# The last pair of blocks as seven products, its last product leaving its bank in groups of 128 tokens, the rest stored by column halves

## The chip, the cores and the metric

The kernel runs on one core of one Trainium2 chip. The metric is the device time of one execution in microseconds (us). "Span" is the length of one profiled execution as the trace shows it; it is 1.7 us shorter than the device time of the same execution (380.3 for 382.04 us before the change). Engines: PE is TensorE, DVE is VectorE, ACT is ScalarE, SP issues most of the stores (49 of 51 before the change). In this kernel a matmul's result is put into a bank of PSUM (`ps` in the traces), ACT or DVE copies it from there into an output tile in SBUF (`osb`), and a store, which is a DMA, takes it to `out_dram`. Semaphores are the counters by which the built program makes an engine wait for another engine or for a DMA. A store has landed when the last count of its semaphore has come in.

## The reference, cut

A gated recurrence along time, then a two-armed layer: the larger of two projections, and a projection of that.

```python
# x, f_logit: (4, 6144, 256); lower_bound: (256,); w1, w2: (256, 1024); w_out: (1024, 256)
f = lower_bound + (1 - lower_bound) * sigmoid(f_logit)
for t in range(S):
    h = f[:, t] * h + (1 - f[:, t]) * x[:, t]
    y[:, t] = h
out = np.maximum(y @ w1, y @ w2) @ w_out        # float32, (24576, 256)
```

## The kernel before

The 24576 tokens are 48 blocks of 512. The maximum is written as `w1·y + relu((w2 - w1)·y)`, so that a block's output is a sum over ten slices of 128: four slices of relu and one of `y` for each half `k` of the features. Two blocks `ja`, `jb` make a pair. With the ten slices in two halves (5 and 5) and the 256 output columns in two halves (`lo`, `hi`), a pair's output is a 2x2 by 2x2 matrix product, and all middle pairs do it with seven products instead of eight (Strassen's way). Each product is 20 matmuls of 128 columns: 4 groups of 128 tokens times 5 slices. The sums on the left side (`sum1` to `sum4`) are made by DVE from the relu's results.

This is the order of the seven, cut. `bank` is a bank of PSUM of 128x512 floats, `X`, `B` and `E` are three of them. `then` gives what follows a product's last matmul: `seed` and `snapshot` are copies by ACT, `leave` is a copy by ACT or a sum by DVE into the output tile.

```python
def sevenths(p):
    ...
    def seed(b, src):                       # new bank b = copy of bank src
        open_bank(b); nc.scalar.copy(out=bank[b][:], in_=bank[src][:])
    def snapshot(b, name):                  # to SBUF
        t = snpool.tile(...); nc.scalar.copy(out=t[:], in_=bank[b][:]); snap[name] = t
    def leave(b, j, cols, name, last):
        dst = osbs[j][:, :, cols]
        if name is None: nc.scalar.copy(out=dst, in_=bank[b][:])
        else: nc.vector.tensor_tensor(out=dst, in0=bank[b][:], in1=snap[name][:], op=ALU.add)
        if last: store(j, osbs[j])          # 512 KB, 4 KB pieces
    ...
    product("X", part(0, 0), plain(0, lo), True)
    then(seed("B", "X"))
    product("E", sub(1), given(t1), True)
    then(snapshot("E", 5))
    product("X", sub(2), given(t2))
    then(snapshot("X", 2))
    product("B", part(0, 1), plain(1, lo))
    then(leave("B", ja, lo, None, False))
    product("X", sub(3), given(t3))
    then(leave("X", jb, hi, 5, False))
    product("E", sub(4), plain(1, hi))
    then(leave("E", ja, hi, 2, True))
    product("X", part(1, 1), given(t4))
    then(leave("X", jb, lo, None, True))
```

A pair's products run in the gaps of the first layer of the next pair. The last pair has no next one, so the kernel before does it by the plain second layer, ten matmuls of 256 columns for each group. For the last block each group has a bank of its own and leaves at once:

```python
def second_layer(j, slot):
    ...
        if s == 0 and (r == 0 or j == NBLK - 1):
            acc["ps"] = ps_o.tile([P, 2, D], FP32, name="ps")     # a new bank
    ...
        if j == NBLK - 1 and s == n - 1:
            (nc.vector.tensor_copy if r else nc.scalar.copy)(
                out=osb[:, i : i + 1, :], in_=ps[:, r : r + 1, :])
            store(j, osb, i, 1, nc.sync if r else nc.scalar)      # 128 KB
...
for step in queue:                       # what is left of the pair before
    step()
for j in (NBLK - 2, NBLK - 1):
    for slot in range(FC):
        second_layer(j, slot)
```

## Time and profile before

| | before |
|---|---|
| device time, median of 4 runs | 382.45 us (382.36 to 382.71) |
| span of the profiled run | 380.3 us |
| PE busy | 97% of the span |
| last 80 matmuls (256 columns) | 367.20 to 376.12 us |
| last copy ends | 376.56 us |
| from there to the end | 3.70 us |

The page of the profile, part 4 (the chain of work that ended last, shares of the span):

```profile
PE 91%; DVE 6%; DMA 1%; ACT 0%; issue 0%; SPq 0%
```

PE is the bound. The end of that chain, as the chain of waits in order of time has it (start us, length us, what):

```profile
365.97 1.40 PE ps L605 x25
367.37 8.75 PE ps L482 x80
376.11 0.02 issue
376.14 0.42 DVE osb L491
```

In each line a group of instructions has its start, its length, its engine, the tile that it writes, its line of the kernel and its count. L605 is the matmul of the seven products, L482 that of the plain second layer. For 8.75 us PE does the last pair and nothing else; the change is about these 80 matmuls. From the timeline, the matmuls that give the rates (start us, length us, engine, line, operation, tiles, shapes, count):

```profile
366.09 1.28 PE L605 MATMUL ps<-t,r 128*128 128x128 f16 x20
367.20 0.38 PE L482 MATMUL ps<-w,r 128*128 128x256 f16 x2
...
376.14 0.42 DVE L491 COPY osb<-ps 128x256 f32<-128x256 f32 x1 [1.76 <-PE ps L482]
```

Twenty matmuls of 128 columns start within 1.11 us (366.09 to 367.20), 55.6 ns each. The costs of what stands around the products, from the page's groups (after the bar: busy us, mean ns of one):

```profile
L506 DVE TENSOR_TENSOR S<-r,S 128x2560 f16<-128x2560 f16 x42 | 62.0, 1477 | 0.0
L562 DVE TENSOR_TENSOR osb<-ps,sn 128x512 f32<-128x512 f32 x42 | 28.7, 684 | 6.5 <-ACT osb L560 5.3
L550 ACT COPY sn<-ps 128x512 f32<-128x512 f32 x42 | 24.6, 586 | 1.1 <-PE ps L605 1.1
```

So a late sum is 1.48 us, a sum out of a bank 0.68, a copy of a whole bank 0.59.

### The profile page before, as it was taken

To read this page: it belongs to the slowest core of one execution; us is meant where nothing else is said; L and a number is where in the kernel's file an instruction comes from. 1 tells how busy PE (TensorE), PEld (TensorE's weight loads), DVE (VectorE), ACT (ScalarE), POOL (GpSimd) and SP (SyncE) were. 2 spreads that over 40 slices of the span, in tenths; PEclk is the share of its full clock that TensorE was granted. 3 is DMA by queue.
4 is the path that set the end of the run, shared out by engine and by line. 5 is a ranking of instruction groups with operands and counts; after the bars stand their busy time and mean duration, and the time that the engine had idled before them with its cause. 6 is when DMAs were issued, how large, how long until landed. Compare 5 with 4: busy or idle time off the path is not lost.

```text
span 380.3 us, 9454 instructions
## 1 busy us (share of the span) xinstructions
PE 369.3 (97%) x4076; PEld 280.0 (74%) x4076; DVE 332.9 (88%) x402; ACT 300.4 (79%) x406; POOL 39.4 (10%) x79
## 2 busy tenths in 40 slices
PE   5999998999999999999999999999999999999995
PEld 4677766777777777777777777777777777777784
DVE  5685789999999999999999999999999999999721
ACT  5856797798798888888887887988888888888740
POOL 1500101110210110101201100202201101000000
PEclk9999999999999999999999999999999999999999
DMA  7995989999989999999999989999899999950223
GB/s 253 245 229 124 309 138 215 262 192 172 296 160 198 307 197 158 267 163 225 224 181 262 267 149 221 237 161 283 156 214 259 171 222 274 174 214 4 110 113 113
DMA packets 103389, 77.17 MB, mean 203 GB/s; under 512 B 93554, under 2 KB 94066, under 8 KB 102642
## 3 DMA queue, kind: packets, MB, share of 16 engines
q1 hardware_dynamic: 100514, 51.13, 60.0%
q0 software_dynamic: 2544, 25.17, 34.0%
q8 instruction: 32, 0.52, 0.6%
q10 hardware_dynamic: 288, 0.26, 0.2%
q14 instruction: 11, 0.09, 0.1%
HBM read 53.48 MB, written 48.23 MB: 267 GB/s over the span
## 4 chain that ended last, share of the span: by engine, by line
PE 91%; DVE 6%; DMA 1%; ACT 0%; issue 0%; SPq 0%
PE ps L605 42%; PE dT L436 41%; PE ps L482 6%; DVE r L230 1%; DVE S L506 1%; DMA osb<-in_f_logit_dram 1%; DVE wd L360 1%; PE ps L180 1%; DVE v L223 1%; DVE r L264 1%; DVE ff L213 0%; DVE t L415 0%; PE ps L392 0%; DVE osb L496 0%; ACT r L444 0%
## 5 line engine op out<-in xcount | busy, mean ns | idle before, releaser
L444 ACT ACTIVATE r<-dT 128x1024 f16<-128x1024 f32 x192 | 195.8, 1022 | 54.4 <-PE dT L436 54.3
L436 PE MATMUL dT<-r,wd 128*128 128x512 f16 x768 | 225.5, 379 | 1.1 <-ACT r L444 0.5
L605 PEld LDWEIGHTS <-S 128*128 128x128 f16 x1680 | 110.9, 101 | 38.6 <-DVE S L506 1.2
L605 PEld LDWEIGHTS <-r 128*128 128x128 f16 x1260 | 87.3, 101 | 36.6
L230 DVE TENSOR_TENSOR_SCAN r<-ff,r,v 128x512 f16<-128x512 f16 x88 | 108.2, 1271 | 0.8
L605 PE MATMUL ps<-t,S 128*128 128x128 f16 x1260 | 97.8, 219 | 1.0 <-DVE S L506 1.0
L436 PEld LDWEIGHTS <-wd 128*128 128x128 f16 x768 | 67.6, 113 | 6.5 <-issue 1.2
L506 DVE TENSOR_TENSOR S<-r 128x2560 f16<-128x2560 f16 x42 | 62.4, 1487 | 10.3 <-ACT r L444 10.3
L605 PE MATMUL ps<-wob,r 128*128 128x128 f16 x672 | 67.4, 219 | 0.0
L506 DVE TENSOR_TENSOR S<-r,S 128x2560 f16<-128x2560 f16 x42 | 62.0, 1477 | 0.0
L285 ACT ACTIVATE u<-fT 128x512 f16<-128x512 f16 x88 | 56.0, 637 | 0.6 <-DMA fT<-scr 0.6
L348 POOL CAST waited<-fT 128x1 f32<-128x1 f16 x21 | 13.6, 649 | 279.7 <-DMA fT<-scr 279.7
L213 DVE TENSOR_SCALAR ff<-u,nom 128x512 f16<-128x512 f16 (+1 forms) x98 | 31.4, 346 | 10.6 <-ACT u L207 6.7
L605 PE MATMUL ps<-w,r 128*128 128x128 f16 x168 | 36.8, 219 | 0.0
L562 DVE TENSOR_TENSOR osb<-ps,sn 128x512 f32<-128x512 f32 x42 | 28.7, 684 | 6.5 <-ACT osb L560 5.3
L605 PE MATMUL ps<-t,r 128*128 128x128 f16 x420 | 33.4, 219 | 0.0
L605 PE MATMUL ps<-wob,S 128*128 128x128 f16 x336 | 31.4, 219 | 0.0
L223 DVE TENSOR_TENSOR v<-u,xT 128x1024 f16<-128x1024 f16 x44 | 30.2, 686 | 0.0
L482 PEld LDWEIGHTS <-r 128*128 128x128 f16 x240 | 23.9, 101 | 6.9
L482 PE MATMUL ps<-wob,r 128*128 128x256 f16 x192 | 26.8, 273 | 0.0
L550 ACT COPY sn<-ps 128x512 f32<-128x512 f32 x42 | 24.6, 586 | 1.1 <-PE ps L605 1.1
L560 ACT COPY osb<-ps 128x512 f32<-128x512 f32 x42 | 24.4, 581 | 0.5 <-PE ps L605 0.5
(56 smaller groups left out, 134.3 us busy)
## 6 DMA issues: line engine op xcount, KB each, us to landing
out_dram<-osb SPq DMA_DIRECT2D x47, 512.0 KB, 3.8
scr<-in_f_logit_dram POOLq DMA_DIRECT2D x22, 512.0 KB, 7.8
scr<-in_x_dram POOLq DMA_DIRECT2D x22, 512.0 KB, 10.6
r<-in_moe_w_dram SPq DMA_DIRECT2D x4, 512.0 KB, 6.8
fT<-in_f_logit_dram POOLq DMA_DIRECT2D x3, 256.0 KB, 8.2
xT<-in_x_dram POOLq DMA_DIRECT2D x3, 256.0 KB, 9.7
osb<-in_f_logit_dram SPq DMA_DIRECT2D x2, 256.0 KB, 3.6
osb<-in_x_dram SPq DMA_DIRECT2D x2, 256.0 KB, 3.6
```

What stands on the lines that cost most here:

```text
L213: nc.vector.tensor_scalar(out=ff[:, h, cols], in0=u[:, h, cols], scalar1=nom[:, h : h + 1], scalar2=1.0, op0=ALU.mult, op1=ALU.add,)
L223: nc.vector.tensor_tensor(out=like(v[:, :, cols], xT), in0=like(u[:, :, cols], xT), in1=xT, op=ALU.mult,)
L230: nc.vector.tensor_tensor_scan(out=y_of(j, h), data0=ff[:, h, o : o + TB], data1=v[:, h, o : o + TB], initial=0.0 if t0 == 0 else y_of(j - ...
L285: nc.scalar.activation(out=mids[p + NBLK, "u"][:, h, cols], in_=held[c, 0][:, h, cols], func=AF.Sigmoid, scale=-1.0,)
L436: nc.tensor.matmul(dT[:, fc % 2, :], lhsT=wd[:, kc, unit_cols(fc)], rhs=y_of(j, kc), start=(kc == 0), stop=(kc == KC - 1),)
L444: nc.scalar.activation(out=rts[j, k][:, g - 1 : g + 1, :].rearrange("p q (i m) -> p q i m", m=P), in_=dT[:].rearrange("p q (m i) -> p q i ...
L482: nc.tensor.matmul(ps[:, r, :], lhsT=left, rhs=right, start=(s == 0 and (r == 0 or j == NBLK - 1)), stop=(s == n - 1 and (r == 1 or j == N ...
L506: nc.vector.tensor_tensor(out=t[:], in0=a, in1=b, op=op)
L550: nc.scalar.copy(out=t[:], in_=bank[b][:])
L560: nc.scalar.copy(out=dst, in_=bank[b][:])
L562: nc.vector.tensor_tensor(out=dst, in0=bank[b][:], in1=snap[name][:], op=ALU.add)
L605: nc.tensor.matmul(bank[b][:, i, :], lhsT=a[:, k, cols], rhs=w, start=fresh, stop=after is not None, skip_group_check=True,)
```

## The change

The intent: 140 matmuls of 128 columns in place of 80 of 256 (the work of seven eighths), with the end trimmed. Product B is moved forward, where it can run while DVE makes the sums; the last product leaves in four groups so that the last copy and store are small; the outputs of a half of the columns are stored as soon as they are there. Cut to its core:

```diff
     def sevenths(p):
+        end = p == NPAIR - 1
@@ leave
-                if last:
+                if end:
+                    store(j, osbs[j], cols=cols)          # 256 KB, 512 B pieces
+                elif last:
                     store(j, osbs[j])
+        def leave_group(b, j, cols, i):
+            def go():
+                copy, queue = (
+                    (nc.vector.tensor_copy, nc.sync),
+                    (nc.scalar.copy, nc.scalar),
+                )[i % 2]
+                copy(out=osbs[j][:, i, cols], in_=bank[b][:, i, :])
+                store(j, osbs[j], slice(i, i + 1), cols, queue)   # 64 KB
+            return go
@@ the seven
+        def first_out():
+            product("B", part(0, 1), plain(1, lo))
+            then(leave("B", ja, lo, None, False))
         product("X", part(0, 0), plain(0, lo), True)
         then(seed("B", "X"))
+        if end:
+            first_out()
         product("E", sub(1), given(t1), True)
         then(snapshot("E", 5))
         product("X", sub(2), given(t2))
         then(snapshot("X", 2))
-        product("B", part(0, 1), plain(1, lo))
-        then(leave("B", ja, lo, None, False))
+        if not end:
+            first_out()
         ...
         product("X", part(1, 1), given(t4))
-        then(leave("X", jb, lo, None, True))
+        if end:
+            for i in range(TB // P):                       # the last matmul of each group
+                steps[(i - TB // P + 1) * (KH + 1) - 1][-1] = leave_group("X", jb, lo, i)
+        else:
+            then(leave("X", jb, lo, None, True))
@@ sum3 of the last pair is made in the loop too; the tail of the kernel
-        for j in (NBLK - 2, NBLK - 1):
-            for slot in range(FC):
-                second_layer(j, slot)
+        steps = sevenths(p)
+        for step in steps[:20]:
+            step()
+        sum1(p); sum2(p); sum4(p)
+        for step in steps[20:]:
+            step()
```

The special cases for the last block in `second_layer`, its banks and its copies, go.

More of the change, by code (lines that the diff above doesn't have):

```diff
@@ L450, in first_layer, with store @@
             )
-    def store(j, osb, first=0, n=TB // P, queue=None):
+    def store(j, osb, groups=slice(0, TB // P), cols=slice(0, D), queue=None):
         b, t0, nb, c, o = blocks[j]
@@ L456, in store @@
             out=out[r0 : r0 + nb, :].rearrange("(p n) d -> p n d", p=P)[
-                :, first : first + n, :
+                :, groups, cols
             ],
-            in_=osb[:, first : first + n, :],
+            in_=osb[:, groups, cols],
         )
@@ L470, in second_layer @@
             g, r = divmod(i, 2)
-            if s == 0 and (r == 0 or j == NBLK - 1):
+            if s == 0 and r == 0:
                 acc["ps"] = ps_o.tile([P, 2, D], FP32, name="ps")
@@ L485, in second_layer @@
                 rhs=right,
-                start=(s == 0 and (r == 0 or j == NBLK - 1)),
-                stop=(s == n - 1 and (r == 1 or j == NBLK - 1)),
+                start=(s == 0 and r == 0),
+                stop=(s == n - 1 and r == 1),
                 skip_group_check=True,
             )
-            if j == NBLK - 1 and s == n - 1:
-                (nc.vector.tensor_copy if r else nc.scalar.copy)(
-                    out=osb[:, i : i + 1, :], in_=ps[:, r : r + 1, :]
-                )
-                store(j, osb, i, 1, nc.sync if r else nc.scalar)
-            elif r == 1 and s == n - 1:
+            if r == 1 and s == n - 1:
                 (nc.scalar.copy if j == 0 else nc.vector.tensor_copy)(
@@ L713 @@
             more = p + 1 < NPAIR
-            seq = [(27, scans[p]["scan10"]), (36, scans[p]["scan11"])]
+            seq = [
+                (27, scans[p]["scan10"]),
+                (36, scans[p]["scan11"]),
+                (112, lambda: sum3(p)),
+            ]
             if more:
@@ L721 @@
                     (84, scans[p + 1]["scan01"]),
-                    (112, lambda: sum3(p)),
                     (131, scans[p + 1]["decay1"]),
@@ L753 @@
             step()
-        for j in (NBLK - 2, NBLK - 1):
-            for slot in range(FC):
-                second_layer(j, slot)
+        p = NPAIR - 1
+        steps = sevenths(p)
+        for step in steps[:20]:
+            step()
+        sum1(p)
+        sum2(p)
+        sum4(p)
+        for step in steps[20:]:
+            step()
 _INS = ['x', 'f_logit', 'lower_bound', 'moe_w1', 'moe_w2', 'moe_w_out']
```

## The prediction

> **What bounds the kernel now.** TensorE: the chain of waits puts 91% of the 380.3 us span on PE. The tail is the last pair of blocks. In the timeline the seven-product work of the pair before ends with 20 matmuls of 128 columns from 366.09 us. Then 80 matmuls of 256 columns (the plain second layer) run from 367.20 to 376.12, 109 ns apart. The last copy (128x256, DVE, 0.42) ends at 376.56, the span 3.74 us later, with the last store. In the window 367 to 376 DVE is busy for 1.8 us, ACT for 1.3.
>
> **Removed and added on PE.** 80 x 109 ns = 8.75 us go. 7 x 20 matmuls of 128 columns come, at 55.6 ns (the 20 from 366.09; the Trainium skill, "TensorE: Matmul & The Clock Gate", Back-to-back issue gap, gives the same): 7.8 us. The change wins 1.0 us if PE never waits.
>
> **But it will wait, as the order of the built program shows.** From the trace: copy of a 128x512 bank on ACT 0.58, DVE sum with a snapshot 0.69, a matmul ends 0.22 after its start, a release costs about 0.05 each way.
> 1. Product B now follows its seed at once: last X matmul ends 368.48, seed 368.53 to 369.10, B starts 369.16. Lost: 0.85 us. In earlier pairs two products lie between.
> 2. With B moved forward, X's third product follows the snapshot of X at once: another 0.85 us.
> 3. The last product's four groups share one bank, and the first matmul of each waits for the copy of the group before (the Trainium skill, "PSUM — Partial Sum Buffer", PSUM bank collisions, asks for guarding by bank, not address; this trace has no such case). The old tail gave each group its own bank. A 128x128 copy is about 0.28 us (estimate from 0.42 and 0.69 on DVE, 0.37 and 0.59 on ACT for 256 and 512 columns). A group takes 0.22 + 0.22 + 0.05 + 0.28 + 0.06 = 0.83 us instead of 0.28, and the first copy queues on DVE behind the sum of E. Copies end at about 376.8, 377.6, 378.4, 379.25.
>
> The three late DVE sums (1.48 each) are not the limit: the last relu ends at 366.9, so they are done at 368.5, 370.0, 371.4, and wanted at 370.3, 371.4, 374.5. The sum added in the loop falls where DVE idles (5.3 us before 364.36).
>
> **Sum.** The last copy ends at 379.25 instead of 376.56: +2.7 us, all on the critical path. The rest stays near 3.7 us: the store is 64 KB instead of 128, on ACT's queue (2.4 us to landing there before, 2.0 on SP); the halves' stores in 512 B pieces should have landed. 382.47 + 2.7 = 385.2 us, 0.7% slower.
>
> **What would show it.** PE waits (view of waits): about 0.85 us on the seed and on the snapshot, one near 1 us and two near 0.55 on the 128x128 copies; none on DVE sums; copies of about 0.28 us; a last copy near 379.2; windows up to 366 us unchanged; granted clock 1.0 but for the end.
>
> **What would make it wrong.** The 512 B pieces may clog the DMA queues, so that the last store lands late (up to +1 us). PE's half-idle end may lower its clock (+0.3 us a group). Or waits are shorter than estimated; without any, the time is 381.5.
>
> Chances: faster by over 2% 0.01, within 2% 0.97, slower 0.02. Range 383.8 to 386.6.

## The result

| | before | after |
|---|---|---|
| device time, median of 4 runs | 382.45 us | 384.27 us (384.22 to 385.71) |
| ratio to before | | 1.0056 (95%: 1.0032 to 1.0079) |
| span of the profiled run | 380.3 us | 382.4 us |
| last copy ends | 376.56 us | 379.26 us |
| from there to the end | 3.70 us | 3.19 us |

The change makes the kernel 0.5% slower by the medians, a loss clear of the noise (the interval of the ratio leaves out 1), which counts as the same at the threshold of 2%. Ratios here and below are the mean time of one kernel's fast runs over that of the other's of the same rounds, so not quite the ratio of the medians that are quoted.

Everything up to the tail is as it was. The same stretch in the view of windows, before and then after (stretch, its length, busy us and counts of PE, PEld, DVE, ACT, POOL, granted clock, DMA share, GB/s):

```profile
340.00:366.00 26.00, 26.00 (x308) 19.83 (x307) 19.12 (x21) 20.80 (x28) 0.00 (x0) 1.00 0.16 63
```

```profile
340.00:366.00 26.00, 26.00 (x306) 19.82 (x305) 20.59 (x22) 20.71 (x28) 0.00 (x0) 1.00 0.16 64
```

PE is busy throughout in both; DVE has one instruction more (`sum3`, 1.5 us), and it delays nothing. The loss is in the tail. The chain of waits after the change (start us, length us, what):

```profile
368.66 0.58 ACT ps L540
...
369.28 3.52 PE ps L623 x60
...
372.82 0.59 ACT sn L546
...
375.89 0.69 DVE osb L558
376.58 0.21 DVE osb L573
...
376.83 0.45 PE ps L623 x5
...
379.00 0.27 ACT osb L573
```

Where before one line of PE was 8.75 us long, the chain now leaves PE for ACT at the seed (L540), for ACT at the snapshot (L546), for DVE at the sum of E (L558) and then after each five matmuls for a copy (L573). The timeline of the last product, PE and its copies (in brackets: idle time before it, and who ended it):

```profile
375.69 0.44 PE L623 MATMUL ps<-t,r 128*128 128x128 f16 x5
...
376.50 0.28 DVE L573 COPY osb<-ps 128x128 f32<-128x128 f32 x1
376.83 0.44 PE L623 MATMUL ps<-t,r 128*128 128x128 f16 x5 [0.70 <-DVE osb L573]
...
377.31 0.27 ACT L573 COPY osb<-ps 128x128 f32<-128x128 f32 x1 [3.90 <-PE ps L623]
...
377.63 0.44 PE L623 MATMUL ps<-t,r 128*128 128x128 f16 x5 [0.35 <-ACT osb L573]
...
378.17 0.29 DVE L573 COPY osb<-ps 128x128 f32<-128x128 f32 x1 [1.39 <-PE ps L623]
378.52 0.44 PE L623 MATMUL ps<-t,r 128*128 128x128 f16 x5 [0.45 <-DVE osb L573]
```

PE and the copies take turns: the program makes each group wait for the semaphore of the copy before it. Groups start 1.14, 0.80 and 0.89 us apart, where five matmuls take 0.28. The idle times in brackets are shorter than the loss, because a matmul counts as busy for 0.22 us and the next one could have started 0.16 us before that end.

For the rest it helps to cut each run's tail into three terms, because the start of the kernel varies from run to run (the mark below stands between 366.98 and 368.66 us in the runs). The tail can be compared without it: in the three runs whose program is the same up to the last copy, the kernel before and the two with added loads, that copy ends 9.52 us behind the mark each time. The starting mark is the issue of the first of the two last 512 KB stores of the pair before; it stands at 367.04 us before and at 367.12 after, 0.95 us behind the first of that pair's last 20 matmuls in both. All times are those of single records of the trace, and each kernel has one trace; differences of a tenth of a us or two rest on that alone.

| us | mark to last copy's end | to the last store's landing | landing to end | tail |
|---|---|---|---|---|
| before | 9.52 | 1.92 | 1.78 | 13.22 |
| after | 12.14 | 1.62 | 1.57 | 15.33 |

The last copy is 2.62 us later, and 0.51 us of that come back behind it.

### The profile page after: what moved, and what is told of

It is laid out like the page before. It is cut to its first block, busy times and chain, and to the rows that moved or that the text cites. A ratio compares the mean times of both kernels' runs of the same rounds, so it can differ in the third digit from the quotient of the medians.

```text
span 382.4 us, 9593 instructions
## 1 busy us (share of the span) xinstructions
PE 369.0 (96%) x4136; PEld 280.0 (73%) x4136; DVE 338.2 (88%) x406; ACT 302.3 (79%) x410; POOL 40.7 (11%) x79
## 4 chain that ended last, share of the span: by engine, by line
PE 90%; DVE 6%; ACT 1%; DMA 1%; issue 0%; SPq 0%; DVEq 0%; ACTq 0%
PE ps L623 44%; PE dT L436 41%; PE ps L482 4%; DVE r L230 1%; DVE S L501 1%; DMA osb<-in_f_logit_dram 1%; DVE wd L360 1%; PE ps L180 1%; DVE v L223 1%; DVE r L264 1%; DVE t L415 0%; DVE ff L213 0%; PE ps L392 0%; DVE osb L491 0%; ACT r L444 0%
## 5 line engine op out<-in xcount | busy, mean ns | idle before, releaser
L623 PEld LDWEIGHTS <-S 128*128 128x128 f16 x1760 | 115.4, 101 | 39.4 <-issue 1.4
L623 PEld LDWEIGHTS <-r 128*128 128x128 f16 x1320 | 90.9, 101 | 39.3 <-issue 2.7
L623 PE MATMUL ps<-t,S 128*128 128x128 f16 x1320 | 101.4, 219 | 1.7 <-DVE S L501 1.0
L501 DVE TENSOR_TENSOR S<-r 128x2560 f16<-128x2560 f16 x44 | 65.4, 1486 | 14.6 <-ACT r L444 14.5
L623 PE MATMUL ps<-wob,r 128*128 128x128 f16 x704 | 69.8, 219 | 0.7 <-ACT ps L540 0.7
L501 DVE TENSOR_TENSOR S<-r,S 128x2560 f16<-128x2560 f16 x44 | 64.9, 1475 | 0.0
L623 PE MATMUL ps<-w,r 128*128 128x128 f16 x176 | 38.5, 219 | 0.0
L623 PE MATMUL ps<-t,r 128*128 128x128 f16 x440 | 35.2, 219 | 1.5 <-DVE osb L573 1.2
L558 DVE TENSOR_TENSOR osb<-ps,sn 128x512 f32<-128x512 f32 x44 | 30.1, 684 | 4.7 <-PE ps L623 4.7
L546 ACT COPY sn<-ps 128x512 f32<-128x512 f32 x44 | 25.8, 586 | 2.2 <-PE ps L623 2.2
L482 PEld LDWEIGHTS <-r 128*128 128x128 f16 x160 | 16.0, 101 | 6.2
L623 PE MATMUL ps<-w,S 128*128 128x128 f16 x88 | 19.3, 219 | 0.0
```

What stands on the lines that cost most here:

```text
L482: nc.tensor.matmul(ps[:, r, :], lhsT=left, rhs=right, start=(s == 0 and r == 0), stop=(s == n - 1 and r == 1), skip_group_check=True,)
L501: nc.vector.tensor_tensor(out=t[:], in0=a, in1=b, op=op)
L623: nc.tensor.matmul(bank[b][:, i, :], lhsT=a[:, k, cols], rhs=w, start=fresh, stop=after is not None, skip_group_check=True,)
```

## The experiments

Each run is compared with the kernel before on the same chip. The tail is that of its profiled run; the difference of the medians agrees with the difference of the tails within 0.3 us in every run.

| run | median, this and before | ratio (95%) | mark to copy | to landing | to end | tail |
|---|---|---|---|---|---|---|
| one copy | 383.12, 382.14 | 1.0026 (1.0014 to 1.0038) | 10.48 | 2.70 | 0.92 | 14.10 |
| B late | 383.26, 382.14 | 1.0035 (1.0022 to 1.0049) | 10.91 | 1.62 | 1.60 | 14.13 |
| both | 382.01, 382.14 | 1.0000 (0.9988 to 1.0013) | 9.25 | 2.78 | 0.92 | 12.95 |
| two banks | 383.57, 382.14 | 1.0045 (1.0032 to 1.0058) | 10.57 | 2.40 | 1.74 | 14.71 |
| no seed | 383.43, 382.17 | 1.0040 (1.0028 to 1.0052) | 11.26 | 1.62 | 1.60 | 14.48 |
| last on SP | 384.02, 382.17 | 1.0054 (1.0041 to 1.0067) | 11.88 | 1.61 | 1.57 | 15.06 |
| full rows | 384.80, 382.17 | 1.0067 (1.0055 to 1.0079) | 12.13 | 1.97 | 1.77 | 15.87 |
| combined | 382.33, 382.17 | 1.0010 (0.9998 to 1.0022) | 9.14 | 2.41 | 1.72 | 13.27 |
| before + 7 loads | 381.66, 382.21 | 0.9989 (0.9975 to 1.0004) | 9.52 | 2.01 | 0.89 | 12.42 |
| before + 8 loads | 381.89, 382.21 | 0.9993 (0.9981 to 1.0005) | 9.52 | 2.05 | 1.34 | 12.91 |
| combined, first block whole | 382.20, 382.21 | 1.0008 (0.9992 to 1.0025) | 9.14 | 2.82 | 1.33 | 13.29 |
| the same, sum in halves | 382.69, 382.21 | 1.0011 (0.9998 to 1.0024) | 8.83 | 3.59 | 1.35 | 13.77 |

In the two runs with loads the profile's view names no landing of the last store; there the time at which SP passes the wait for it is taken, which is 0.02 us behind the semaphore's last count.

### One copy

```diff
-        if end:
-            for i in range(TB // P):
-                steps[(i - TB // P + 1) * (KH + 1) - 1][-1] = leave_group("X", jb, lo, i)
-        else:
-            then(leave("X", jb, lo, None, True))
+        then(leave("X", jb, lo, None, True))
```

> The changed kernel, but its last product leaves its bank in one copy and one store, as in the earlier pairs (undoes the groups alone). Theory (the four groups in one bank make PE wait for each copy): the 20 last matmuls run unbroken from 375.7 to 377.0, one ACT copy of 0.58 ends at 377.6 instead of 379.26; the store is now 256 KB and lands about 1 us later than a 64 KB one, so the span falls by about 0.5 us, from 382.4 to about 381.9. Rival (the groups hide the copy as they were meant to, and the loss is all in the two stalls on ACT): without groups the span rises by about 0.5 us or more.

The end of the chain of waits of this run:

```profile
373.78 3.52 PE ps L619 x60
...
377.33 0.59 ACT osb L556
```

The last three products run unbroken, and one copy of the whole bank ends 1.66 us earlier (10.48 behind the mark for 12.14). The theory holds and the rival falls: the groups put the last copy off by 1.66 us, for a store of 64 KB that lands 1.08 us sooner than one of 256 KB. Not expected was the last column: landing to end is 0.92 us and no longer 1.57. That made the gain 1.23 us instead of 0.5, and opened a second question, taken up below.

### B late

```diff
-        if end:
-            first_out()
         product("E", sub(1), given(t1), True)
         ...
-        if not end:
-            first_out()
+        first_out()
```

> The changed kernel, but product B stands where it stands in the earlier pairs, after the second X product (undoes the move alone). Theory (the move opens the two stalls of 0.87 and 0.84 us in PE's starts, on the seed and on the snapshot of X): both vanish; but PE comes to the DVE sums earlier than they are ready, about 0.15 us at sum 1 and 0.35 at sum 2. The span falls by about 1.2 us to 381.2. Rival (the move is needed because the sums would cost as much): the span stays within 0.3 us of 382.4.

The chain of waits, cut to the part before the last product:

```profile
366.08 1.03 ACT r L444
...
367.14 2.91 DVE S L501 x2
...
370.09 4.66 PE ps L620 x80
```

Both stalls are gone: 80 matmuls follow each other. In their place the chain runs through the last relu and two DVE sums: the second X product starts at 370.09, the moment sum 2 is done. With no wait it would have started 40 matmuls behind the first X product's start at 367.39, at about 369.6. So the sums cost about half a microsecond and the two stalls cost 1.7; the copies end 1.23 us earlier. The move of B does cover the sums, as it was meant to, but at three times their price.

### Both

Both edits above together, which is how the earlier pairs are done.

> Both undone: the last pair is done just as the earlier ones, but the halves are stored apart. Theory: the two savings add up to about 1.7 us, span about 380.7, about 0.1% above the kernel before (380.3). If they overlap (what is won earlier is lost at the end), it is clearly less than the sum.

The copy ends 2.89 us earlier than after the change: 1.66 + 1.23, so the two losses are separate and add up. The kernel is then as fast as before, not faster (ratio 1.0000), though PE does 1 us less work. About 0.5 us goes to the DVE sums and 0.17 to a larger last copy (0.59 us for 0.42), so that the copy ends only 0.27 us before that of the old kernel; the 256 KB store lands 0.86 us later than the old one of 128 KB, and a shorter end (0.92 us for 1.78) gives just that back.

### Two banks

```diff
+        def second_bank():
+            open_bank("Y")
+            nc.scalar.copy(out=bank["Y"][:, 2:4, :], in_=bank["X"][:, 2:4, :])
         product("X", sub(3), given(t3))
-        then(leave("X", jb, hi, 5, False))
+        # leave("X", jb, hi, 5, False), then second_bank()
         ...
         product("X", part(1, 1), given(t4))
-        # four groups out of X
+        # the last 10 matmuls go to Y; X's half leaves by DVE, Y's by ACT, 128 KB each
```

> The changed kernel, but the second half of the last product goes to a bank of its own, which ACT first fills from X's half, and each half leaves in one copy, by DVE and by ACT. Theory (the waits of the end come from one bank being shared, not from copies or stores as such): no PE wait on a copy between the halves; the fill delays the first by about 0.3 us; the last copy ends at about 377.7 instead of 379.26 and the span is about 381.2 (1.2 us less). Rival (copies on two engines during PE's writes, or the stores, are what costs): no gain over the run with one copy (381.9).

The end of the chain of waits:

```profile
374.69 0.70 DVE osb L558
...
375.42 0.37 ACT ps L579
...
375.82 1.29 PE ps L642 x20
...
377.18 0.37 ACT osb L584
```

With a bank for each half the twenty matmuls of the last product run through (1.29 us), while DVE copies the first half out of the other bank. So neither the copies nor DVE's reading at the same time holds PE; only the shared bank did, by the waits that the program puts there. Whether the chip would bear the groups without these waits, no run tried. The last copy is 1.57 us earlier, as expected. The gain in the tail is only 0.62 us, because the 128 KB store lands 0.78 us later than the 64 KB one, and the end is 0.17 longer; the verdict on the span (1.2 us) was wrong for that reason, and on the copy right. By the yardstick that was set, the span, the rival came out: there is no gain over the run with one copy (tail 14.71 for 14.10 us). On PE it is refuted, but its "or the stores" stands.

### No seed

```diff
         product("X", part(0, 0), plain(0, lo), True)
-        then(seed("B", "X"))
+        then(snapshot("X", 0) if end else seed("B", "X"))
         ...
-            product("B", part(0, 1), plain(1, lo))
-            then(leave("B", ja, lo, None, False))
+            product("B", part(0, 1), plain(1, lo), end)        # in an empty bank
+            then(leave("B", ja, lo, 0 if end else None, False))  # DVE adds the snapshot
```

> The changed kernel, but product B of the last pair starts in an empty bank and does not wait for a seed: ACT copies X to SBUF beside it, and DVE adds that copy when B leaves. Theory: the stall of 0.87 us on the seed goes and nothing takes its place (sum 2 is ready at 370.0 and now wanted at 370.6; the added DVE sum comes after the three sums, in idle time): span 381.5 to 381.6. Rival (PE would then wait for the DVE sums instead): PE waits on sum 1 or sum 2 by some 0.5 us and the span falls by less than 0.4.

The chain of waits up to the one stall that is left before the last product, on the snapshot:

```profile
365.95 5.99 PE ps L623 x107
...
371.97 0.59 ACT sn L546
```

The copy ends 0.88 us earlier, and in the tail PE shows no wait for a DVE sum. The stall on the seed is worth what it looked like, and it is avoidable at no cost that this run shows: a copy that the next product needs is turned into one that only the leaving needs.

### Last on SP, and full rows

The first swaps the engines of the groups (`)[i % 2]` to `)[1 - i % 2]`), the second stores full rows again (`if end: store(j, osbs[j], cols=cols)` goes, and a group stores 256 columns, 128 KB).

> The changed kernel with the parity of the groups swapped: groups 0 and 2 leave by ACT, 1 and 3 by DVE and the SP queue, so that the last store is issued by SP as before the change. The time from the last copy to the end was 3.70 us before and 3.19 after. If the smaller last store (64 KB for 128) explains it, it stays at 3.1 to 3.3; if ACT's queue does, it goes back to about 3.5 to 3.7. Besides, group 0 no longer queues on DVE behind the sum of E, so the last copy should end about 0.4 us earlier (378.85).

> The changed kernel, but stored by full rows: the first block whole when both halves are there, the second by groups of 256 columns (undoes the stores by column halves alone). Theory: PE and the copies are unchanged (last copy at 379.26); the last store is 128 KB again and lands 1.9 us after its issue instead of 1.6: span about 0.3 us longer. Rival (the many 512 B pieces clog the queues): the span gets shorter.

The last store's time to landing, from the view of the store's line in the stretch of the last issue. Issued by SP with 64 KB:

```profile
DMA to landing us min/median/max: 1.6/1.6/1.6
```

Issued by ACT with 128 KB (full rows):

```profile
DMA to landing us min/median/max: 1.9/1.9/1.9
```

The size decides (64 KB 1.6 us on either queue, 128 KB 1.9 on either: SP before, ACT here), not the queue. (The pieces, 512 B and 1 KB, change with the size, so the two are not told apart.) The smaller last store is the one part of the change that was shown to pay: 0.3 us. With full rows the tail grew by 0.54 us, more than the 0.3 expected, because the last store had the first of the eight semaphores again (the section on the seven and eight loads explains these): 1.77 us from landing to end in place of 1.57. The copies of "last on SP" end 0.26 us earlier, less than the 0.4 expected; the first copy no longer queues behind DVE's sum, but DVE had begun it at 376.50 already, before that sum's end at 376.58.

### Combined

A version to beat both: no seed; B's first half before the sums are wanted and its second half after the second X product, so that it covers the snapshot; the last product in two banks.

```diff
         product("X", part(0, 0), plain(0, lo), True)
+        # snapshot 0 of X;  B, first 10 matmuls, in an empty bank
         product("E", sub(1), given(t1), True)
         product("X", sub(2), given(t2))
+        # B, last 10 matmuls
         product("X", sub(3), given(t3))       # then the second bank Y
         product("E", sub(4), plain(1, hi))
         product("X", part(1, 1), given(t4))   # halves in X and Y
```

> A version to beat both: B without a seed, its first half before the sums are wanted and its second half between the snapshot of X and its use; the last product in two banks. Estimate from the trace: left-over waits about 0.3 us at the snapshot and 0.2 at the fill, PE ends at 375.8, last copy at 376.2 (before 376.56, after 379.26), span about 379.7, 0.6 us under the kernel before. If the DVE sums or DVE's longer work at the end bind, PE shows waits on the sums or the last copy comes after 376.6.

Its last copy ends 3.00 us earlier than after the change and 0.38 earlier than before; the estimate for the copy was right (a left-over wait of about 0.27 us at the snapshot and one at the fill). The time is that of before all the same (ratio 1.0010, 0.9998 to 1.0022): the last store lands in 2.37 us from its issue instead of 1.89, at the same 128 KB, though in pieces of 512 B and no longer of 1 KB. What the DMA engines moved, in 40 slices of 0.16 us from 374 to 380.5 us:

```profile
GB/s 0 0 0 0 19 262 290 296 287 290 167 3 22 277 287 293 284 280 167 136 299 265 315 277 281 300 293 274 287 293 202 10 0 0 0 0 0 0 0 0
```

From 376.0 us to 379.1 they move 512 B pieces at about 285 GB/s with one dip, and the last store, issued at 377.06, comes at the end of that. More output is left to store at the very end than before; the last two runs make that plainer.

### What follows the last landing: seven and eight loads

"One copy" had shown that the end after the landing is not fixed. SP's own records (time in us at which a wait is passed; the last store's semaphore is marked), before and in "one copy":

```text
before     378.50* 378.56 378.63 378.72 378.79 378.86 378.93 379.30  then end 380.26
one copy   378.59 378.66 378.72 378.81 378.89 379.27 379.55 380.64*  then end 381.54
```

SP waits for eight DMA semaphores in a fixed order. They are given out in turn, so the count of DMAs decides which one the last store has. Before it is the first, and six steps of 0.06 to 0.09 us and a longer one of 0.37 come after the landing; in "one copy" it is the last, and the others were passed during the transfer. The test adds loads of 64 B to the kernel before, in the middle of the loop, that nothing uses:

```diff
+            if p == PAIR0 + 5:
+                for pad in pads:             # 7 in one run, 8 in the other
+                    nc.sync.dma_start(out=pad[:], in_=lower_bound.rearrange(
+                        "(h p) -> h p", h=1)[:, 0:16])
```

> The kernel before, with seven 64 B loads added on the SP queue in the middle of the kernel (nothing uses them). Theory of the end: after the last store has landed, SP still passes the waits for the other DMA semaphores in a fixed order, and the eight of them are given out in turn, so the number of DMAs decides how many waits are left: 1.78 us from landing to end before (first of eight), 1.57 after the change (third), 0.92 in the run with one copy (last). Seven more DMAs make the last store's the last of the eight: the end comes 0.8 to 0.9 us earlier (ratio about 0.998) although work was added. Rival (the end is as long as it is for other reasons, size or queue of the last store): no gain.

> Control of the run above: eight loads instead of seven, which gives the last store its old semaphore back. Theory: within 0.1 us of the kernel before, 1.78 us from landing to end. Rival (loads in the middle shift something else): both runs with loads move alike.

With seven loads the tail is 0.80 us shorter, as expected, though work was added. The control was not clean: with eight the last store has its old semaphore again, but the tail is 0.31 us shorter too. The waits behind the landing are all there and take 0.06 us each; the longer step of 0.37 us is missing from them. It stands elsewhere in SP's order in each kernel (after the seventh wait in the kernel before, ahead of the first wait with seven loads), so it moves with the number of SP's instructions; what it is, no run shows. The order of the semaphores is thus worth the difference of the two runs, 0.45 us, and not 0.8. The timed runs cannot tell the two apart (0.9989 and 0.9993, with overlapping intervals). "Before with seven loads" has the lowest median of all, but its interval reaches 1.0004, so it isn't shown to be faster either.

### Combined, with the first block whole, and with the sum in halves

The first stores block `ja` in one piece, when its last half is there. The second also makes the sum that leaves X before the last product in two halves, the second out of Y.

> The combined version, with the first block stored whole, which is one DMA fewer and gives the last two stores the last two semaphores. PE and copies as in the combined version. Theory: 0.6 to 0.8 us under the combined version (from landing to end about 1.0 instead of 1.72), so 0.6 us under the kernel before. Rival (the number of stores by itself is nothing): no change.

> The same, with the sum before the last product done in two halves, so that DVE leaves the bank X 0.27 us sooner and the left-over PE wait at the fill of the second bank goes. Estimate: PE's end, last copy and span another 0.25 us earlier; 0.8 to 0.9 us under the kernel before. If DVE's four additions and copies at the end bind instead, nothing is won.

Both got what they were built for and lost it in the stores. With the first block whole, the end after the landing is 0.39 us shorter and the landing 0.41 later. With the sum in halves, the last three products run through without a wait, and the last copy comes at 8.83, the earliest of all runs, 0.69 us before that of the kernel before:

```profile
372.07 3.52 PE ps L657 x60
...
375.62 0.37 ACT osb L595
```

But its last store takes 3.56 us to land and the tail is 0.55 us longer than before. The stores' line in the stretch from 374.5 us of this run, and the DMA view's GB/s in 40 slices of 0.16 us from 374 to 380.5 us:

```profile
DMA to landing us min/median/max: 2.7/3.3/3.6
```

```profile
GB/s 0 0 0 0 0 0 0 0 0 0 0 41 280 293 284 296 287 457 407 403 403 353 302 403 403 287 259 284 287 284 284 155 3 0 0 0 0 0 0 0
```

The DMA engines work without a gap for 3.4 us, until the last byte. Four stores, 1 MB in all, are issued within 1.4 us (374.6 to 376.0). The slices between 376.8 and 378.1 us, mostly near 400 GB/s, are the 512 KB of the first block in pieces of 4 KB; those before and behind, near 285, are the second block in pieces of 512 B. This is the DMA row of the same stretch of the kernel before:

```profile
GB/s 353 429 403 284 303 365 133 95 353 322 82 25 6 0 265 334 208 0 0 0 0 284 347 177 0 0 0 0 0 0 0 0 0 0 0 0 50 0 0 0
```

There the last block's groups leave 1.1 us apart, and 640 of the pair's 1024 KB have landed by 376.2 us. With seven products in this order no quarter of the output is complete before the fourth product (in the changed kernel, where B stands second, one is stored at 371.25 us), and three quarters come with the last three. So the order of the products moves stores to the end, and once PE's waits are gone the stores bind. A rival for part of it was not tested: the pieces. By an estimate from the two rates of this row, the second block's 512 KB at 285 in place of 400 GB/s cost some 0.5 us, about as much as the 0.55 that this run lost. A version without PE's waits that stores full rows was not run.

## Why the prediction was right, point by point

The device time was predicted at 385.2 us (range 383.8 to 386.6), the verdict at "within 2%"; measured were 384.27 and the same verdict. 2% is 7.6 us and the whole tail is 13 to 15; what tests the prediction are the waits, one by one.

1. "80 x 109 ns go, 7 x 20 matmuls of 55.6 ns come, a win of 1.0 us if PE never waits": right. The unbroken chains keep that rate (60 matmuls in 3.52 us, the last one's 0.22 included), and the version with nearly no waits ends its copies 0.69 us before the kernel before, with about 0.3 us of wait left.
2. "Product B follows its seed at once: 0.85 us": right. B starts 0.93 us after the last X matmul in place of 0.06: 0.87. Taken away alone, it gives 0.88.
3. "X's third product follows the snapshot: another 0.85": right, 0.84. "B late" takes 2 and 3 away together and gives 1.23, after DVE sums of about 0.5.
4. "The groups share one bank, 0.83 us for a group": right. Starts 0.80 and 0.89 apart, and 1.14 for the first, which queued on DVE behind the sum of E as said. Copies 0.28, 0.27, 0.29, 0.27 (predicted 0.28). "One copy" and "two banks" show that it is the shared bank. The sizes in the view of waits came out lower than predicted (0.7 for 0.85), because that view counts from the modelled end of the matmul before.
5. "The DVE sums are not the limit", "the sum added in the loop falls where DVE idles": right; no PE wait on them is new.
6. "The last copy ends at 379.25": measured 379.26. That it fits to 0.01 us is partly luck: this run's mark stands 0.08 us later than the one that the forecast was worked out from; from the mark, 12.21 were forecast and 12.14 measured.
7. "The rest stays near 3.7 us": this is the term that was mis-sized; it was 3.19. The prediction weighed the smaller size against the other queue and let them cancel. The queue is worth nothing, the size 0.3 us, and 0.2 us came behind the landing, where SP has five waits left in place of seven (0.15 us) and the steps after the last wait are 0.05 us shorter; the prediction did not consider this at all. The feared clogging by 512 B pieces did not happen in this kernel; in the versions with less waiting the last store did land late, how much of it for the pieces no run separates. PE's granted clock stayed at 1.00 up to 379 us, so the pauses between the groups cost no clock.

The remaining 0.4 us of the difference is the base: the tail was forecast from the profiled run of before, which took 382.04 us, and added to 382.47, the median of that kernel's first three runs. The two profiled runs differ by 2.18 us, the tails by 2.11, the medians by 1.82.

## What to carry to other kernels

A form that saves matmuls did not pay at the end of this kernel with the order of release that it was given, and no variant tried was shown to be faster than the kernel before: draw the tail as a chain (last matmul, copy, store, landing, end) and check each new neighbour of a copy for a wait, and each pair of steps that shares a PSUM bank, because in this program PE and the copying engine take turns on a bank however small the pieces are. Cutting the last copy and store into pieces is no gain if the pieces share a bank: here it put the last copy off by 1.66 us for a landing 1.08 us sooner. And before optimizing the last microsecond of PE, look at what is left to store then, and in what pieces: once the waits were gone, the stores took back all of it.

## What the Trainium skill lacked or had wrong

- "DMA: Bandwidth & Descriptors", Specifications, has 512 B as the smallest transfer for full rate. Here stores in pieces of 512 B moved at about 285 GB/s with the engines busy, stores in pieces of 4 KB mostly at about 400 (the first of the two DMA rows of the last experiment, where both occur). For these stores that row of the page is too lenient.
- The same page, Anatomy of one DMA, gives a fit of 2.0 us plus the bytes over 436 GB/s, for the software queue. It has no such fit for the hardware queues of SP and ACT, only a time to the first byte; here the last store landed 1.59 us after its issue at 64 KB (512 B pieces) and 1.89 at 128 KB (1 KB pieces) when nothing else moved much, by these two points less fixed time and more for each byte.
- "Runtime: NRT & Kernel Launch", The ~15µs preamble/postamble breakdown, lists what the runtime puts behind a kernel; what the program itself does between its last landing and its end is on none of the pages read: 0.89 to 1.78 us here, of which 0.45 us depends only on the order in which SP passes the waits for eight DMA semaphores.
- "PSUM — Partial Sum Buffer", PSUM bank collisions raise a hardware error, asks for guarding by bank and quadrant, or more simply by bank. The built program makes PE wait where a copy reads another part of the same bank, but the page has no price for it: a group of five matmuls and its copy in one bank came every 0.80 to 0.89 us, where the matmuls alone are 0.28.
- "TensorE: Matmul & The Clock Gate", Back-to-back issue gap, gives N/2.4 + 2.5 ns for an isolated matmul of N columns, which is 55.8 for 128, but about 81 ns as the sustained rate in a stream of weight loads and matmuls. This trace keeps 55.6 ns with a weight load for every matmul (20 of each from 366.09 us).
